# Output product with its engines in a written order, and one load moved a product earlier

## The chip, the cores and the metric

The kernel runs on one core of a Trainium2 chip. The metric is device time in microseconds of one execution of the whole program. Before the change the median of three runs is 2396.21 us, the lowest 2393.97 and the highest 2399.01. Everything is computed in 32-bit floats; matrix products are made of several passes of a faster 32-bit format, as told below.

## The reference

One input `x` of 2048 rows and 1024 columns goes through two branches that a gate per row mixes:

```
g = sigmoid((x * gate_w).sum(-1))
q, k, v = x @ wqkv, 32 heads of 32
phi(t) = [softmax(t @ w_phi), softmax(-(t @ w_phi))]          per head
kv = phi(k)^T v ;  z = sum over rows of phi(k)
o  = phi(q) kv / (phi(q) . z + 1e-6)
a  = o @ wo                                     1024 x 1024
b  = (gelu(x @ w_gate) * (x @ w_up)) @ w_down   1024 -> 3584 -> 1024
out = g * a + (1 - g) * b
```

The last products, `o @ wo` and `h @ w_down`, are summed straight into one output of 2048 x 1024. The kernel scales the attention's rows by `g` before its product, so that product is added with a plain sign, while the MLP's results are scaled by `1 - g` (`g_b`, and `g_n` with the sign turned) in the add.

## The kernel before

A product of two 32-bit matrices is made of three matmuls. Each operand is split into a *high* part (ScalarE copies it into the matmul's format; helper `high`, or the first line of `split`) and a *low* part (VectorE subtracts the high part from the original; `low`, or the second line of `split`); the passes are high x high, high x low and low x high (`PASSES`). So before an operand of 128 x 1024 can be used it needs one load by SyncE's DMA queue (SP), one ScalarE instruction and one VectorE instruction.

The kernel has three stages. The first projects keys and values and accumulates `kv` and `z`. The second, the **unit stage**, makes the queries, gates and ups. The third, the **output product**, multiplies with `wo` and `w_down`.

*Unit stage* (lines 438 to 949). Rows are taken in two halves of 1024. A unit is two 128-column blocks of one weight matrix (kind g, u or q) against one half. It is done as seven products of 12 matmuls (as in Strassen's scheme) with operands that are sums of blocks; they are called x, y, z and v on the weight side. `unit` emits one product per slot, and after each product `run_slot(t)` lets generators emit other engines' work. A generator yields (earliest slot, deadline, VectorE cost, ScalarE cost); among those that may go, the one with the earliest deadline goes first, and without a passed deadline it goes only while the slot's budget of 2.65 us lasts. All of TensorE, VectorE, ScalarE and SP stand in this written order. Staging buffers are taken in a rotation of four by `hold`, and `room(n)` says whether the next n are free.

`weights` is the generator for one unit's weight operands. Sums of weight blocks ("T sums") are made in the first half, stored by `right_sums` in memory, and read back in the second half: the first of them with the unit's first loads, the second (line 597, tile names tq, tg and tu) with a yield of its own on line 594. `second_half` replaces the x operands while the halves change; its loads (line 521) have four staging buffers and are read back from `xs` or from the input. `first_rights` prepares the first two right operands of the output product in the last unit.

*Output product* (lines 952 to 1037). For each of seven products `i` (in the order `ORDER`), first the attention part (2 steps of the contraction per half of the rows), then the MLP part (7 steps per half). A *turn* is one product for one half and one part: four accumulation banks, filled over 2 or 7 steps. A *step* is 24 matmuls: a left operand of 128 x 1024 (high and low) against a right operand of 128 x 1024 (high and low), in four row blocks. There are 28 turns and 126 steps. The order of the two halves alternates, so that a right operand is used in two turns.

- `left` (line 985) loads one block or two into `stage` and `sl`, adds or subtracts them on VectorE (line 992), and splits the result into one of three slots: two named wgu and one named wl.
- `right` (line 957) does the same with rows of `wo` or `w_down`, staged in three buffers named sr, into one of ten slots (three named tyz, seven named tw). `make_right` makes at most one per step, in the MLP part at every other step.
- `add_into` (line 1000) empties the banks of a finished turn: with ScalarE copies the first time a block of the output is reached (line 1007), else with VectorE adds (lines 1010 and 1012), all of them marked urgent. Where a block is finished, it is stored (line 1014).

In this stage only TensorE's order is written (`manual_schedule(engines={PE})`). The order on VectorE, ScalarE and SP is chosen by the framework's planner, which may also move work ahead into the end of the unit stage, and which puts urgent instructions first. Banks alternate between two sets of four: a turn needs the banks of the turn two before it to be empty.

Of the kernel before, what the change touches and what calls it, by code (L numbers as in the profile page):

```python
# [8 lines left out]
F32 = mybir.dt.float32  # L9
F32R = mybir.dt.float32r  # L10
# [6 lines left out]
P = 128  # L17
# [14 lines left out]
def tile_gated_mix(ctx: ExitStack, tc: tile.TileContext, x, xT, wkT, wqT, wv, w_phi, wo,  # L32
# [9 lines left out]
    def split(dst_h, dst_l, src):  # L42
        nc.scalar.activation(dst_h, src, AF.Copy)  # L43
        nc.vector.tensor_tensor(dst_l, src, dst_h.bitcast(F32), OP.subtract)  # L44

    def stage(*parts, pool=None, into=None):
        t = into
        if t is None:
            t = (pool or ring).tile([P, 1024], F32, tag="stage", name="stage", bufs=1 if pool else 3)
        for o, n, src in parts:  # L50
            nc.sync.dma_start(t[:, o:o + n] if len(src.shape) == 2 else
                              t[:, o:o + n].rearrange("p (a b) -> p a b", a=src.shape[1]), src)
        return t
# [7 lines left out]
    def urgent():  # L61
        return tc.high_priority(offset=URGENT)
# [370 lines left out]
    def right_block(src, at, d):  # L433

        r, c = at
        return src[4 * d * P:4 * (d + 1) * P, c * BLK:(c + 1) * BLK].rearrange("(m r p) n -> r p m n", r=2, p=P)[r]

    with tc.tile_pool(name="xa", bufs=1) as xa, tc.tile_pool(name="fp", bufs=1) as fp, \
# [8 lines left out]
        def start(gen):  # L447
            streams.append([next(gen), len(streams), gen])
# [98 lines left out]
        def weights(n, half, kind, m):  # L547
# [369 lines left out]
        def first_rights(t):  # L917

            for d in range(N_ATT):
                yield t + 1 + 3 * d, t + 1 + 3 * d, 0.0  # L920
                while not room(2):
                    yield now[0] + 1, now[0] + 1, 0.0
                a, *b = RIGHT[ORDER[0]]
                k1, s1 = hold((0, 1024, right_block(wo, a, d)))
                k2, s2 = hold((0, 1024, right_block(wo, b[0], d)))
                yield max(now[0] + 2, t + 3 + 4 * d), t + 7, 1.25, 1.05
                w = slot().rearrange("p a b c -> p a (b c)")
                nc.vector.tensor_tensor(s1, s1, s2, OP.add if b[1] == 1 else OP.subtract)
# [4 lines left out]
                made.append(w.rearrange("p a (m n) -> p a m n", m=2))  # L933

        jobs = []
        for n, (half, kind, m) in enumerate(units):
            if n:
# [2 lines left out]
                jobs += [(7 * (n + 1) + 3, half, 2 * m + i // 2, i % 2) for i in range(4)]  # L940
        start(background(jobs, 7 * next(n for n, u in enumerate(units) if u[0])))
        start(first_rights(7 * len(units) - 7))
        start(late_lows())
        for n, u in enumerate(units):
            unit(n, *u, units[n - 1] if n else None)
# [4 lines left out]


    fours = [ctx.enter_context(tc.tile_pool(name=f"po{n}", bufs=4, space=PSUM)) for n in range(2)]
    with tc.tile_pool(name="op", bufs=1) as op, tc.manual_schedule(engines={PE}):
        acc = [ring.tile([P, 4, D], F32, name=f"x{n // 2}{n % 2}", bufs=1) for n in range(4)]
        SLOTS, MID = N_MLP, 3

        def right(src, i, d, pool, tag, bufs):

            w = pool.tile([P, 2, 2, BLK], F32R, tag=tag, name=tag, bufs=bufs)
            a, *b = RIGHT[i]  # L960
            s = stage_right((0, 1024, right_block(src, a, d)))
            if b:
                t = stage_right((0, 1024, right_block(src, b[0], d)))
                nc.vector.tensor_tensor(s, s, t, OP.add if b[1] == 1 else OP.subtract)  # L964
            split(w[:, 0].rearrange("p a b -> p (a b)"), w[:, 1].rearrange("p a b -> p (a b)"), s)
            return w

        def stage_right(*parts):
            t = op.tile([P, 1024], F32, tag="sr", name="sr", bufs=3)
            for o, n, src in parts:  # L970
                nc.sync.dma_start(t[:, o:o + n].rearrange("p (a b) -> p a b", a=src.shape[1]), src)
            return t

        def make_right():

            k = len(made)
            if k < len(rights) and k < used + MID + SLOTS:
                mlp, i, d = rights[k]
                pool, tag, bufs = (mid, "tyz", MID) if k % (MID + SLOTS) < MID else (op, "tw", SLOTS)
                made.append(right(w_down if mlp else wo, i, d, pool, tag, bufs))  # L980

        slots = itertools.cycle((new_weight, new_weight,
                                 lambda: op.tile([P, 2, KC, P], F32R, tag="wl", name="wl", bufs=1)))

        def left(src, i):

            a, *b = LEFT[i]
            s = stage((0, 1024, src[a]))
            if b:
                t = op.tile([P, 1024], F32, tag="sl", name="sl", bufs=2)  # L990
                nc.sync.dma_start(t.rearrange("p (a b) -> p a b", a=2), src[b[0]])
                nc.vector.tensor_tensor(s, s, t, OP.add if b[1] == 1 else OP.subtract)  # L992
            w = next(slots)().rearrange("p a b c -> p a (b c)")
            split(w[:, 0], w[:, 1], s)
            return w.rearrange("p a (m n) -> p a m n", m=2)

        def banks(n):
            return [fours[1 - n % 2].tile([P, BLK], F32, tag="po", name="po") for _ in range(4)]

        def add_into(i, half, ps, mlp, done, last):  # L1000
            for r, col, sign in INTO[i]:
                for c in range(4):
                    row = half * 8 + r * 4 + c
                    part = acc[row // 4][:, row % 4, col * BLK:(col + 1) * BLK]
                    with urgent():
                        if (half, r, col) not in done:
                            nc.scalar.activation(part, ps[c], AF.Copy, scale=float(sign))
                        elif mlp:
                            gate_c = (g_b if sign == 1 else g_n)[:, row:row + 1]
                            nc.vector.scalar_tensor_tensor(part, ps[c], gate_c, part, op0=OP.mult, op1=OP.add)  # L1010
                        else:
                            nc.vector.tensor_tensor(part, part, ps[c], OP.add if sign == 1 else OP.subtract)
                    if (r, col) in last:
                        nc.sync.dma_start(out[row * P:(row + 1) * P, col * BLK:(col + 1) * BLK], part)
                done.add((half, r, col))

        done = set()
        turn = used = 0
        for n, i in enumerate(ORDER):
            for mlp, lefts, n_duo in ((0, left_att, N_ATT), (1, left_mlp, N_MLP)):  # L1020
                last = {t[:2] for t in INTO[i]} - {t[:2] for j in ORDER[n + 1:] for t in INTO[j]} if mlp else set()
                first = used
                for second, half in enumerate((0, 1) if turn % 4 == 0 else (1, 0)):
                    ps = banks(turn)
                    turn += 1
                    for d in range(n_duo):
                        ls = left(lefts[half][d], i)
                        if not mlp or (second * n_duo + d) % 2 == 0:
                            make_right()
                        for m in range(2):  # L1030
                            for c in range(4):
                                for k, (a, e) in enumerate(PASSES):
                                    nc.tensor.matmul(ps[c], ls[:, a, m, c * P:(c + 1) * P], made[first + d][:, e, m],  # L1033
                                                     start=d == 0 and m == 0 and k == 0,
                                                     stop=d == n_duo - 1 and m == 1 and k == 2)
                        used += second
                    add_into(i, half, ps, mlp, done, last)


# [33 lines left out]
```

## Time and profile before

| what | value |
|---|---|
| median of three runs | 2396.21 us |
| the profiled execution's own time | 2396.52 us |
| its span, first to last instruction | 2394.7 us |
| TensorE busy | 2378.0 us, 99% |
| VectorE busy | 1746.9 us, 73% |
| ScalarE busy | 991.4 us, 41% |
| GpSimd busy | 141.6 us, 6% |
| output product, first to last matmul start | 1697.08 to 2390 us |

Times in rows are microseconds from the span's start. A row of the timeline has the start, the time taken, the engine (SPq and POOLq are queues that issue transfers), the line of the kernel, the operation, written tile <- read tiles, shapes, and the count of merged instructions; in brackets, how long the engine was idle before it and what ended that. Matmuls are pipelined: each record lasts about 389 ns, and the next begins before it ends.

### The profile page before, as it was taken

Reading aid. Unit: us, or ns where it says so; the run is one execution under the profiler, and the core shown is the slowest. Engines: PE = TensorE matmul, PEld = TensorE weight load, DVE = VectorE, ACT = ScalarE, POOL = GpSimd, SP = SyncE. Lnnn points to the kernel's source line nnn. Section 1 sums busy time; section 2 is a strip of 40 time slices with the busy share of each in tenths; the row PEclk is TensorE's granted clock in tenths of the full one; section 3 lists DMA queues with packets and bytes.
Section 4 is the critical chain, followed back from the end, with each engine's and each line's share of the span. In section 5 each row is a group of like instructions: output and inputs, shape, how many; then the busy total and the mean of one; then the engine's idle time right before and its main releaser. Section 6 shows DMA issues by size and latency. Waiting matters only on the chain.

```text
span 2394.7 us, 28170 instructions
## 1 busy us (share of the span) xinstructions
PE 2378.0 (99%) x10689; PEld 1973.8 (82%) x10689; DVE 1746.9 (73%) x2183; ACT 991.4 (41%) x1286; POOL 141.6 (6%) x266
## 2 busy tenths in 40 slices
PE   9999999999999999999999999999999999999999
PEld 8888888788888888878888888888887888888887
DVE  7877868857777777877767676777565778677773
ACT  4323332435445444555555555555433323223221
POOL 0000000011111112100000000000000000000000
PEclk9999999999999999999999999999999999999999
DMA  5112333544544566474444444434686667878873
GB/s 178 45 47 86 97 115 100 183 171 144 184 171 142 189 217 225 155 255 138 137 138 156 142 133 139 150 133 141 236 278 205 234 229 271 297 277 290 282 261 131
DMA packets 154360, 425.10 MB, mean 178 GB/s; under 512 B 21360, under 2 KB 21360, under 8 KB 154224
## 3 DMA queue, kind: packets, MB, share of 16 engines
q1 hardware_dynamic: 127872, 336.64, 42.4%
q0 software_dynamic: 25312, 86.52, 9.4%
q8 instruction: 84, 1.38, 0.2%
q14 instruction: 52, 0.43, 0.1%
q10 hardware_dynamic: 1040, 0.13, 0.0%
HBM read 328.34 MB, written 94.90 MB: 177 GB/s over the span
## 4 chain that ended last, share of the span: by engine, by line
PE 71%; DMA 4%; issue 3%; DVE 2%; ACT 0%; POOL 0%; SPq 0%; DVEq 0%; POOLq 0%; ACTq 0%
PE po L1033 24%; PE a L744 19%; PE c L744 13%; PE p L744 6%; PE b L744 6%; DMA sr<-in_w_down 2%; PE misc L906 2%; DVE sr L964 1%; DMA sr<-in_wo 1%; DVE x L1010 1%; DMA stage<-tq 0%; DMA raw<-xs 0%; POOL lm L135 0%; DVE tyz L424 0%; DMA lm<-h 0%
## 5 line engine op out<-in xcount | busy, mean ns | idle before, releaser
L200 PE MATMUL pd<-wkv,x 128*128 128x512 f32 x1536 | 362.0, 393 | 0.0
L200 PEld LDWEIGHTS pd<-wkv,x 128*128 128x128 f32 x1536 | 285.4, 188 | 58.2 <-issue 1.0
L1033 PE MATMUL po<-tw,wgu 128*128 128x512 f32 x1344 | 310.1, 389 | 1.0 <-DVE wgu L44 1.0
L1033 PEld LDWEIGHTS po<-tw,wgu 128*128 128x128 f32 x1344 | 252.3, 188 | 53.6 <-DVE wgu L44 1.4
L43 ACT ACTIVATE wgu<-stage 128x1024 fp32r<-128x1024 f32 x87 | 92.1, 1059 | 237.2 <-PE po L1033 180.8
L744 PE MATMUL a<-s,tyz 128*128 128x512 f32 x744 | 181.2, 392 | 3.1 <-DVE tyz L424 1.6
L424 DVE TENSOR_TENSOR tyz<-stage,tyz 128x1024 fp32r<-128x1024 f32 x126 | 153.0, 1214 | 41.5 <-ACT tyz L421 41.5
L421 ACT ACTIVATE tyz<-stage 128x1024 fp32r<-128x1024 f32 x126 | 132.6, 1052 | 120.3 <-DVE stage L569 65.3
L744 PE MATMUL p<-s,tyz 128*128 128x512 f32 x744 | 178.7, 389 | 0.0
L744 PE MATMUL b<-s,tyz 128*128 128x512 f32 x744 | 178.7, 389 | 0.0
L744 PE MATMUL c<-x,tyz 128*128 128x512 f32 x744 | 178.7, 389 | 0.0
L744 PE MATMUL a<-x,wgu 128*128 128x512 f32 x744 | 178.7, 389 | 0.0
L744 PE MATMUL c<-x,wgu 128*128 128x512 f32 x744 | 178.7, 389 | 0.0
L744 PE MATMUL a<-s,v 128*128 128x512 f32 x744 | 178.7, 389 | 0.0
L992 DVE TENSOR_TENSOR stage<-stage,sl 128x1024 f32<-128x1024 f32 x90 | 109.8, 1225 | 86.1 <-DMA stage<-lm 58.9
L744 PEld LDWEIGHTS a<-s,tyz 128*128 128x128 f32 x744 | 140.4, 189 | 34.2 <-DVE tyz L424 2.9
L744 PEld LDWEIGHTS p<-s,tyz 128*128 128x128 f32 x744 | 139.6, 188 | 29.0
L744 PEld LDWEIGHTS a<-s,v 128*128 128x128 f32 x744 | 139.7, 188 | 29.0
L744 PEld LDWEIGHTS c<-x,wgu 128*128 128x128 f32 x744 | 139.7, 188 | 29.0
L744 PEld LDWEIGHTS c<-x,tyz 128*128 128x128 f32 x744 | 139.7, 188 | 29.0
L744 PEld LDWEIGHTS a<-x,wgu 128*128 128x128 f32 x744 | 139.7, 188 | 29.0
L744 PEld LDWEIGHTS b<-s,tyz 128*128 128x128 f32 x744 | 139.7, 188 | 29.0
(176 smaller groups left out, 3556.0 us busy)
## 6 DMA issues: line engine op xcount, KB each, us to landing
stage<-lm SPq DMA_DIRECT2D x98, 512.0 KB, 4.5
sr<-in_w_down SPq DMA_DIRECT2D x84, 512.0 KB, 4.9
sl<-lm SPq DMA_DIRECT2D x70, 512.0 KB, 4.6
lm<-h POOLq DMA_DIRECT2D x112, 256.0 KB, 2.5
stage<-in_w_gate SPq DMA_DIRECT2D x43, 512.0 KB, 4.2
stage<-in_w_up SPq DMA_DIRECT2D x43, 512.0 KB, 4.3
stage<-la SPq DMA_DIRECT2D x28, 512.0 KB, 4.8
tg<-stage POOLq DMA_DIRECT2D x26, 512.0 KB, 3.0
```

Of the source, the lines that this page charges most:

```text
L43: nc.scalar.activation(dst_h, src, AF.Copy)
L200: nc.tensor.matmul(ps[m], xb[b, kc // 4][:, a, kc % 4, t * P:(t + 1) * P], w[:, e, m * 512:(m + 1) * 512], start=kc == 0 and i == 0, stop= ...
L421: nc.scalar.activation(dst, src, AF.Copy)
L424: nc.vector.tensor_tensor(dst, src, dst_h.bitcast(F32), OP.subtract)
L744: nc.tensor.matmul(dst, w[:, h, 4 * part + kc, :], xq[:, e, kc, :], start=first and kc == 0 and i == 0, stop=kc == 3 and i == 2, skip_grou ...
L906: nc.tensor.matmul(po, kbs[:, a, s, :], pts[:, q, s, :], start=s == 0 and i == 0, stop=s == 1 and i == 2)
L964: nc.vector.tensor_tensor(s, s, t, OP.add if b[1] == 1 else OP.subtract)
L992: nc.vector.tensor_tensor(s, s, t, OP.add if b[1] == 1 else OP.subtract)
L1010: nc.vector.scalar_tensor_tensor(part, ps[c], gate_c, part, op0=OP.mult, op1=OP.add)
L1033: nc.tensor.matmul(ps[c], ls[:, a, m, c * P:(c + 1) * P], made[first + d][:, e, m], start=d == 0 and m == 0 and k == 0, stop=d == n_duo - ...
```

## The change

Two things are changed.

In `weights`, the second T sum of a unit that is not fresh may be loaded from three products ahead of its unit, with a deadline two ahead, where it was two and one.

The output product is rewritten so that TensorE, VectorE, ScalarE and SP all stand in a written order, step by step. A new generator `first_lefts` prepares the first two left operands in the last unit of the unit stage, beside `first_rights`. Before the loop, the loads of lefts 2 to 4 and of two rights are issued. Then each step emits its 24 matmuls and after them: the sum and the high part of the left for two steps later, a load of a left's second term for four steps later, the first right's sum and high part, two adds, the left's low part and the load of a left for five steps later, the rights' remaining parts with two adds between them and one right's load each, and the adds that remain. What a step takes on is chosen by a budget of 5.3 us of VectorE time per step (a wide operation counts 1.25, an add 0.75, a ScalarE copy nothing) and by deadlines: a right must be made two steps before its first use, and a finished turn's adds must be out in the last step before its banks return. A right whose load was issued less than two steps ago is left for later unless it is due. The rights' staging has four buffers where it had three; the three slots of lefts start with wl; adds go bank by bank.

```diff
             if not fresh:
-                yield max(now[0], t - 2), t - 1, 0.0
+                yield max(now[0], t - 3), t - 2, 0.0
...
+        def first_lefts(t):
+            for d in range(2):
+                yield t + 2 + 3 * d, t + 3 + 3 * d, 0.0
+                while not room(1):
+                    yield now[0] + 1, now[0] + 1, 0.0
+                k1, s1 = hold((0, 1024, left_att[0][d][LEFT[ORDER[0]][0]]))
+                yield max(now[0] + 2, t + 4 + 5 * d), t + 7 + 3 * d, 0.0, 1.05
+                w = new_weight()
+                high(flat(w)[0], s1)
+                yield now[0] + 1, now[0] + 1, 1.25
+                low(flat(w)[1], s1, flat(w)[0])
+                held[k1] = False
+                ready.append(Ready(w))
...
-    with tc.tile_pool(name="op", bufs=1) as op, tc.manual_schedule(engines={PE}):
+    with tc.tile_pool(name="op", bufs=1) as op, tc.manual_schedule(engines={PE, DVE, ACT, SP}):
...
+            t = op.tile([P, 1024], F32, tag="sr", name="sr", bufs=4)
...
+        for n in range(2, 5):
+            lefts[n].load()
+        for n in range(2, 4):
+            lefts[n].load_other()
+        for r in todo[:2]:
+            r.load(-1)
...
+            owed = min(owed, 0.0) + STEP
+            nxt = lefts[n + AHEAD] if n + AHEAD < len(steps) else None
+            if nxt:
+                owed -= nxt.cost
+            adds, preps = [], []
+            while True:
+                r = todo[len(preps)] if len(preps) < len(todo) else None
+                if r and (made_of(r.k) > n or r.when >= n - 1 and needed[r.k] - 2 > n):
+                    r = None
+                last_r = needed[r.k] - 2 if r else 10 ** 9
+                last_a = waiting[len(adds)][0] if len(adds) < len(waiting) else 10 ** 9
+                if min(last_r, last_a) == 10 ** 9 or (owed <= 0 and min(last_r, last_a) > n):
+                    break
+                if last_a <= last_r:
+                    a = waiting[len(adds)]
+                    owed -= 0.0 if a[1][6] else 0.75
+                    adds.append(a)
+                else:
+                    owed -= r.cost
+                    preps.append(r)
...
+            if nxt:
+                nxt.first()
+                if n + AHEAD + 2 < len(steps):
+                    lefts[n + AHEAD + 2].load_other()
+            for r in preps[:1]:
+                r.first()
+            some(2)
+            if nxt:
+                nxt.second()
+                if n + AHEAD + 3 < len(steps):
+                    lefts[n + AHEAD + 3].load()
+            for q, r in enumerate(preps):
+                if q:
+                    r.first()
+                    some(2)
+                r.second()
+                if unloaded:
+                    unloaded.pop(0).load(n)
+            some(len(adds))
+            if closes:
+                waiting += [(begins[turn + 2] - 1, a, ps[a[4]]) for a in turns[turn]]
```

Here `first` is the sum (if there are two terms) and the high part, `second` the low part, `some(n)` up to n of the step's adds, `STEP` 5.3, `AHEAD` 2, and `made_of(k)` the first step in which a right's slot is free.

More of the change, by code (lines that the diff above doesn't have):

```diff
@@ L933, in first_rights, with __init__ @@
                 made.append(w.rearrange("p a (m n) -> p a m n", m=2))
+        ready = []
+        def first_lefts(t):
[11 more added lines that the diff above has]
+                ready.append(Ready(w))
+        class Ready:
+            def __init__(self, w):
+                self.out = w.rearrange("p a b c -> p a (b c)").rearrange("p a (m n) -> p a m n", m=2)
         jobs = []
@@ L942, in tile_gated_mix @@
         start(first_rights(7 * len(units) - 7))
+        start(first_lefts(7 * len(units) - 7))
         start(late_lows())
@@ L952, in tile_gated_mix @@
     fours = [ctx.enter_context(tc.tile_pool(name=f"po{n}", bufs=4, space=PSUM)) for n in range(2)]
-    with tc.tile_pool(name="op", bufs=1) as op, tc.manual_schedule(engines={PE}):
+    with tc.tile_pool(name="op", bufs=1) as op, tc.manual_schedule(engines={PE, DVE, ACT, SP}):
         acc = [ring.tile([P, 4, D], F32, name=f"x{n // 2}{n % 2}", bufs=1) for n in range(4)]
[L955 to L971, printed above, removed]
-            return t
[L974 to L1001, printed above, removed]
-                for c in range(4):
[L1003 to L1037, printed above, removed]
@@ new lines, in tile_gated_mix @@
+        turns, steps, lefts, freed, needed = [], [], [], {}, {}
+        done = set()
+        for n, i in enumerate(ORDER):
+            for mlp, srcs, n_duo in ((0, left_att, N_ATT), (1, left_mlp, N_MLP)):
+                last = {t[:2] for t in INTO[i]} - {t[:2] for j in ORDER[n + 1:] for t in INTO[j]} if mlp else set()
+                base = rights.index((mlp, i, 0))
+                for second, half in enumerate((0, 1) if len(turns) % 4 == 0 else (1, 0)):
+                    adds = [(half, r, col, sign, c, mlp, (half, r, col) not in done, (r, col) in last)
+                            for c in range(4) for r, col, sign in INTO[i]]
+                    done |= {(half, r, col) for r, col, _ in INTO[i]}
+                    for d in range(n_duo):
+                        (freed if second else needed)[base + d] = len(steps)
+                        steps.append((len(turns), d, base + d, d == 0, d == n_duo - 1))
+                        lefts.append(ready[len(lefts)] if len(lefts) < len(ready) else Left(srcs[half][d], i))
+                    turns.append(adds)
@@ new lines, in tile_gated_mix @@
+        begins = [next(n for n, s in enumerate(steps) if s[0] == t) for t in range(len(turns))] + [len(steps)] * 2
+        made_of = lambda k: (-1 if k < MID + SLOTS else freed[k - MID - SLOTS]) + 1
+        todo = [Right(k) for k in range(len(made), len(rights))]
+        waiting, banks_of, owed = [], {}, 0.0
+        AHEAD = 2
+        for n in range(2, 5):
[4 more added lines that the diff above has]
+            r.load(-1)
@@ new lines, in tile_gated_mix, with some @@
+        unloaded = todo[2:]
+        for n, (turn, d, k, opens, closes) in enumerate(steps):
+            if opens:
+                banks_of[turn] = [fours[1 - turn % 2].tile([P, BLK], F32, tag="po", name="po") for _ in range(4)]
+            ps, ls, rs = banks_of[turn], lefts[n].out, made[k]
+            for m in range(2):
+                for c in range(4):
+                    for j, (a, e) in enumerate(PASSES):
+                        nc.tensor.matmul(ps[c], ls[:, a, m, c * P:(c + 1) * P], rs[:, e, m],
+                                         start=opens and m == 0 and j == 0, stop=closes and m == 1 and j == 2)
+            owed = min(owed, 0.0) + STEP
[15 more added lines that the diff above has]
+                    adds.append(a)
+                else:
+                    owed -= r.cost
+                    preps.append(r)
+            del waiting[:len(adds)], todo[:len(preps)]
+            def some(count):
+                for _, a, bank in [adds.pop(0) for _ in range(min(count, len(adds)))]:
+                    add_into(*a[:5], bank, *a[5:])
+            if nxt:
[19 more added lines that the diff above has]
+                waiting += [(begins[turn + 2] - 1, a, ps[a[4]]) for a in turns[turn]]
@@ L1041 @@
+        for _, a, bank in waiting:
+            add_into(*a[:5], bank, *a[5:])
 def kernel(A_x, A_wqkv, A_w_phi, A_wo, B_x, B_w_gate, B_w_up, B_w_down, gate_w):
```

57 lines of the change are left out of this document (added).

## The prediction

> **What bounds the kernel now.** I read the page's busy shares first, then TensorE's waits over the whole span.
>
> ```profile
> span 2394.7 us, 28170 instructions
> PE 2378.0 (99%) x10689; PEld 1973.8 (82%) x10689; DVE 1746.9 (73%) x2183; ACT 991.4 (41%) x1286; POOL 141.6 (6%) x266
> PE po L1033 <- DVE wl L44: 3.6, 1, 3.6
> ```
>
> TensorE is the bound, and the change removes no matmul; the longest of its waits, 3.6 us, lies at line 1033, the output product. So a gain can only be time in which TensorE waits or runs slowly. The next view is TensorE's timeline in the output product.
>
> ```profile
> 1697.08 11.04 PE L1033 MATMUL po<-tyz,wgu 128*128 128x512 f32 x48
> ...
> 1762.36 6.05 PE L1033 MATMUL po<-tw,wgu 128*128 128x512 f32 x26
> 1769.38 5.29 PE L1033 MATMUL po<-tw,wgu 128*128 128x512 f32 x22 [0.96 <-DVE wgu L44]
> ...
> 1779.94 11.04 PE L1033 MATMUL po<-tw,wgu 128*128 128x512 f32 x48
> ...
> 1801.70 5.60 PE L1033 MATMUL po<-tyz,wgu 128*128 128x512 f32 x24
> 1808.02 0.70 PE L1033 MATMUL po<-tw,wl 128*128 128x512 f32 x2 [0.71 <-ACT wgu L43]
> 1812.35 6.86 PE L1033 MATMUL po<-tw,wl 128*128 128x512 f32 x22 [3.64 <-DVE wl L44]
> 1819.05 11.04 PE L1033 MATMUL po<-tyz,wgu 128*128 128x512 f32 x48
> ...
> 2384.81 5.60 PE L1033 MATMUL po<-tyz,wl 128*128 128x512 f32 x24
> ```
>
> The undisturbed pace is the difference of two rows: 48 matmuls at 1779.94 take 11.04 us, 24 at 1801.70 take 5.60, so 24 more cost 5.44 us, 0.2267 each; 24 are a step. The output product runs from 1697.08 to 2384.81 + 5.60 = 2390.41, 693.33 us. Its loops make 7 x 18 steps of 24, 3024 matmuls, 685.44 us at that pace, plus 0.16 us by which the last record outlasts its pace. **7.73 us are lost.** Two places hold all of it: 1762.36 to 1779.94 is 17.58 us for 72 matmuls worth 16.32 (1.26 lost), and 1801.70 to 1819.05 is 17.35 us for 48 worth 10.88 (6.47 lost).
>
> The same reading at the start of the unit stage's second half:
>
> ```profile
> 1056.39 2.88 PE L744 MATMUL c<-x,tyz 128*128 128x512 f32 x12
> 1060.30 0.73 PE L744 MATMUL a<-s,tyz 128*128 128x512 f32 x2 [1.03 <-ACT c L777]
> 1062.21 3.99 PE L744 MATMUL a<-s,tyz 128*128 128x512 f32 x10 [1.18 <-DVE tyz L424]
> ...
> 1066.04 2.88 PE L744 MATMUL a<-s,v 128*128 128x512 f32 x12
> ```
>
> 1056.39 to 1066.04 is 9.65 us for two products of 12, worth 5.44: **4.21 us lost.** Not all of it is waiting: the ten matmuls at 1062.21 take 3.99 us where their pace gives 2.43, 1.56 us more. The windows view of TensorE says why (columns after the window: its length, PE busy, granted clock, DMA share, GB/s):
>
> ```profile
> 1062.00:1065.50 3.50, 3.29 (x8) 0.52 0.76 256
> 1812.40:1815.80 3.40, 3.40 (x9) 0.57 0.67 196
> ```
>
> After the waits the granted clock falls to 0.52, and to 0.57 after the one at 1812. A wait of 1 us alone (1769.38) was not followed by such a spell.
>
> The Trainium skill, "TensorE: Matmul & The Clock Gate", part 1, has the clock fall to half "after ≥1 idle window (~3.4µs)" of a free-running window. Here 2.21 us of gaps inside 3.4 us were enough, so the measurement decides: by that rule a new wait of 2 us would cost 2 us, by these rows up to 3.56.
>
> **The change, part by part.**
>
> *(a) Adds spread over steps.* What makes the long stall is visible on VectorE and ScalarE:
>
> ```profile
> 1805.81 1.41 DVE L1010 SCALAR_TENSOR_TENSOR x<-po,g_b,x 128x512 f32<-128x512 f32 x2
> ...
> 1811.08 1.22 DVE L44 TENSOR_TENSOR wl<-stage,wl 128x1024 fp32r<-128x1024 f32 x1
> 1807.84 3.99 ACT L1007 ACTIVATE x<-po 128x512 f32<-128x512 f32 x8
> ```
>
> Eight urgent adds (5.27 us, 0.66 each) stand ahead of the low half of the left operand that the current step needs; the wait at 1769.38 has the same make-up. In the new program a left's low half stands behind at most two adds (1.32 us), it is for two steps later (the three slots free one at the beginning of each step), and the adds have until their banks return. Counting VectorE work per step, with 1.22 us for a wide operation:
>
> ```profile
> L992 DVE TENSOR_TENSOR stage<-stage,sl 128x1024 f32<-128x1024 f32 x90 | 109.8, 1225 | 86.1 <-DMA stage<-lm 58.9 <-DMA stage<-la 14.3 <-DMA sl<-lm 6.2
> ```
>
> a left with two terms costs 2.45, a right with two terms 2.45, four adds 2.64: the heaviest steady steps come to 5.1 to 5.5 us of the 5.44, followed by lighter ones; the early steps 1, 3, 5, 7 and 9 hold a one-term left and two rights, 6.1 us, each followed by 1.2. Nothing accumulates beyond one step, and a left has one step (5.44) in hand. I take both stalls as gone: -7.73. Bounds: -7.73 and, if one stall of the long kind stays, -1.26.
>
> *(b) The order at the beginning* is where I see a price. Queues are now in written order and the output pool still opens only when the last spill has been read:
>
> ```profile
> 1697.89 1.22 DVE L424 TENSOR_TENSOR tyz<-stage,tyz 128x1024 fp32r<-128x1024 f32 x1
> 1699.02 0.68 DVE L719 TENSOR_TENSOR h<-a,x 128x512 f32<-128x512 f32 x1
> 1700.73 0.54 POOL L135 DMA_DIRECT2D lm<-h  x1 [1.92 <-DVE h L721]
> 1703.99 1.41 SPq L971 DMA_DIRECT2D sr<-in_w_down  x3
> 1704.05 1.06 ACT L43 ACTIVATE wl<-stage 128x1024 fp32r<-128x1024 f32 x1 [0.22 <-ACT wgu L43]
> 1705.14 1.22 DVE L44 TENSOR_TENSOR wl<-stage,wl 128x1024 fp32r<-128x1024 f32 x1
> 1709.49 1.23 DVE L964 TENSOR_TENSOR sr<-sr 128x1024 f32<-128x1024 f32 x1 [3.12 <-DMA sr<-in_w_down]
> ```
>
> The second early left's low half falls between the right's low (1697.89) and the unit's last subtraction (1699.02), by the deadlines in the code. Wide operations follow each other by 1.13 us there, so the spill goes at 1701.86, the loads of the rights at 1705.12 and step 2's left is complete at 1707.5; TensorE wants it at 1707.96. The first right's sum comes 5.5 us after its load, 1710.6; behind it, in order, the left of step 3 (done 1713.0, wanted 1713.40), the two rights' remaining halves, the left of step 4 (1718.7, wanted 1718.84), and on ScalarE the eight copies of turn 0 from 1717.3, 0.50 each, to 1721.3. Turn 2 wants their banks at 1718.84, 1719.52, 1720.20 and 1720.88: the last comes 0.4 late. I take **+0.5**. Bounds: 0 (the low half falls behind the subtraction), and +2.8, if the first loads take 7.8 us, as the load in the next fence does, in place of 5.5.
>
> *(c) The second T sums.*
>
> ```profile
> 1045.49 0.46 SPq L51 DMA_DIRECT2D stage<-in_w_up  x1
> 1046.08 1.22 DVE L424 TENSOR_TENSOR tyz<-stage,tyz 128x1024 fp32r<-128x1024 f32 x1
> 1048.46 1.46 SPq L521 DMA_DIRECT2D x<-xs  x2
> 1049.97 0.42 SPq L51 DMA_DIRECT2D stage<-tq  x1
> 1057.76 1.06 ACT L421 ACTIVATE tyz<-stage 128x1024 fp32r<-128x1024 f32 x1 [3.89 <-DMA stage<-tq]
> 1060.94 1.22 DVE L424 TENSOR_TENSOR tyz<-stage,tyz 128x1024 fp32r<-128x1024 f32 x1
> ```
>
> The load at 1049.97 takes 7.8 us; ScalarE stands in it for 3.89 us, and behind that instruction are the copy L777 and the half that VectorE finishes, the two releasers of the stall. One slot earlier, the load's deadline is ahead of those of the two x<-xs loads, so on SP it passes them and goes right behind the one at 1045.49, about 4 us earlier; its buffer is that of four holds back, long free. The passed loads move by one issue, 0.4 us; their highs come after 1060. The stall needs 2 us to vanish: -4.21. In the other units no wait is seen on these loads; the cover is the product by which they already come early. Bounds: -4.21 and 0.
>
> *(d) Loads of rights* gather: in the longest bursts a step fetches a two-term left and a two-term right, four transfers of 0.524 MB, 2.10 MB in 5.44 us or 385 GB/s.
>
> ```profile
> 2100.00:2133.00 33.00, 33.00 (x148) 27.32 (x147) 27.95 (x32) 8.27 (x8) 0.00 (x0) 1.00 0.91 324
> 2200.00:2250.00 50.00, 50.00 (x223) 41.40 (x222) 38.78 (x41) 12.62 (x12) 0.00 (x0) 1.00 0.83 285
> sr<-in_w_down SPq DMA_DIRECT2D x84, 512.0 KB, 4.9
> ```
>
> 324 GB/s at a share of 0.91 is 356 at full share; 2.10 MB then takes 5.89 us, 0.45 over, 1.8 us after a run of four. A right's load has two steps less some 3.5 us, 7.4, against the median 4.9: 2.5 us in hand. So 0; the other bound is the slow rival below.
>
> *(e) The end.*
>
> ```profile
> 2388.41 2.79 DVE L1010 SCALAR_TENSOR_TENSOR x<-po,g_b,x 128x512 f32<-128x512 f32 x4 [11.91 <-PE po L1033]
> ```
>
> The last four adds and stores stay as they are: 0.
>
> **Sum**: 2394.74 - 7.73 - 4.21 + 0.5 = 2383.3 us of span. The profiled execution took 2396.52, 1.8 more than its span, and lies 0.31 above the median 2396.21: 2385.1, so **2384.8 for the median**.
>
> **The rivals.**
> 1. *The early load gains nothing* (it is written behind the second operand's low half and may still come out behind the x<-xs loads): 2384.8 + 4.21 = 2389.0. For it: one generator emits them in sequence. Against: that low half (VectorE, 1046.08) precedes the x<-xs loads.
> 2. *A new stall in the output product*: the start's margins of 0.1 to 0.5 us fail, or a bank's adds come late: 2.3 us (2387.1) up to one stall like that at 1808 (6.47, 2391.3). For it: a right's sum that waits for its transfer now blocks adds and lefts behind it. Against: a step in hand everywhere but at the start.
> 3. *Slower: the bursts become bound by transfers.* At 285 GB/s, 2.10 MB takes 7.37 us, 1.93 over a step. Three runs of three or four such steps, 11 in all, lose 21.2 us less 2.5 in hand for each, 13.7; with a slow spell (1.56) each, 18.4: 2403.2. It is slower than before once the rate in the bursts falls under some 312 GB/s (1.29 over, 11 x 1.29 - 7.5 + 4.7 = 11.4). For it: the 285 above. Against: 324 sustained for 33 us below full share.
>
> **How the numbers follow.** Forecast (all stalls gone, 0 to 2.3 new at the start) 0.62; rival 1 0.12; rival 2 0.17; rival 3 0.06; anything else 0.03. 0.2% is 4.8 us, what a measurement here can tell: faster is below 2391.4. That is the forecast, rival 1 and a third to a half of rival 2, 0.80; the rest of rival 2 with some of "anything else", 0.13, is the same; rival 3 and the remainder, 0.07, slower. Low end: floor 2384.3 (no new loss) less most of what the runs before spread below their median (2.2), 2382.5. High end: rival 2's top with most of that spread, 2393. The likeliest alone: 2383.5 to 2387.5.
>
> **What would show it.** (a) No TensorE gap over 0.3 us after step 12 of the output product, adds in pairs between lefts. (b) The sr loads about 1 us later than 1703.99 relative to the stage's begin, step 2 and 3 barely served, a gap under 1 us at turn 2. (c) stage<-tq ahead of the x<-xs loads, ScalarE without the 3.89 us, granted clock 1.00 there. (d) DMA slices near 350 GB/s without TensorE waits. Wrong is the forecast if waits on sr transfers reach TensorE in the bursts, or if the output product takes more than 688 us from its first matmul to its last.

## The result and the profile after

The changed kernel takes 2384.03 us (median of five runs, 2383.34 to 2384.63) against 2396.21 (five, 2393.06 to 2399.01): a ratio of 0.995, 95% interval 0.9935 to 0.9965, 12.2 us faster. The forecast was 2384.8. The profiled execution took 2383.34 us. The page and TensorE's waits:

```profile
span 2381.5 us, 28170 instructions
PE 2372.2 (100%) x10689; PEld 1969.3 (83%) x10689; DVE 1746.3 (73%) x2183; ACT 991.6 (42%) x1286; POOL 142.2 (6%) x266
...
PE c L703 <- DVE h L651: 1.6, 1, 1.6
...
PE a L744 <- DVE tyz L424: 0.4, 1, 0.4
PE a L744 <- ACT c L777: 0.4, 1, 0.4
```

No wait at the output product stands in this view any more; the rows that remain lie in the first 665 us, which the change does not touch. TensorE's timeline in the output product (line 1088 is what line 1033 was):

```profile
1691.01 11.04 PE L1088 MATMUL po<-tyz,wgu 128*128 128x512 f32 x48
1701.89 5.60 PE L1088 MATMUL po<-tyz,wl 128*128 128x512 f32 x24
1707.33 11.57 PE L1088 MATMUL po<-tyz,wgu 128*128 128x512 f32 x48
1718.74 5.60 PE L1088 MATMUL po<-tw,wl 128*128 128x512 f32 x24
...
2371.54 5.60 PE L1088 MATMUL po<-tyz,wl 128*128 128x512 f32 x24
```

From 1691.01 to 2371.54 + 5.60 it takes 686.13 us where it took 693.33. The one loss is at 1707.33: 11.41 us to the next row for 48 matmuls worth 10.88, **0.53 us**. The start of the second half:

```profile
1043.98 0.46 SPq L51 DMA_DIRECT2D stage<-in_w_up  x1
1044.49 0.42 SPq L51 DMA_DIRECT2D stage<-tq  x1
1046.96 1.46 SPq L521 DMA_DIRECT2D x<-xs  x2
1052.62 1.05 ACT L421 ACTIVATE tyz<-stage 128x1024 fp32r<-128x1024 f32 x1
1054.51 2.88 PE L744 MATMUL c<-x,tyz 128*128 128x512 f32 x12
1057.23 2.88 PE L744 MATMUL a<-s,tyz 128*128 128x512 f32 x12
```

The load of tq passes the two x<-xs loads, ScalarE no longer stands in it, and the products follow at their pace of 2.72 us. Between the same marks of the two timelines:

| stretch | before | after | difference |
|---|---|---|---|
| to the first unit product | 464.20 | 462.69 | -1.51 |
| on to the product c at the second half's start | 592.19 | 591.82 | -0.37 |
| on to the first output matmul | 640.69 | 636.50 | -4.19 |
| output product | 693.33 | 686.13 | -7.20 |
| last matmul to the end | 4.33 | 4.33 | 0 |

The first two rows are not the change. The first comes from the first 20 us, where one execution runs a few more matmuls slowly than another:

```profile
9.17 2.31 PE L200 MATMUL pd<-wkv,x 128*128 128x512 f32 x6
```
```profile
8.19 1.64 PE L200 MATMUL pd<-wkv,x 128*128 128x512 f32 x6
```

The first fence is before, the second after. In another profile of the changed kernel, after_again below, the first unit product begins at 464.23, as before.

### The profile page after: what moved, and what is told of

Read it like the earlier page. It is cut to its first block, busy times and chain, and to the rows that moved or that the text cites. A ratio compares the mean times of both kernels' runs of the same rounds, so it can differ in the third digit from the quotient of the medians.

```text
span 2381.5 us, 28170 instructions
## 1 busy us (share of the span) xinstructions
PE 2372.2 (100%) x10689; PEld 1969.3 (83%) x10689; DVE 1746.3 (73%) x2183; ACT 991.6 (42%) x1286; POOL 142.2 (6%) x266
## 4 chain that ended last, share of the span: by engine, by line
PE 79%; DVE 0%; ACT 0%; issue 0%; ACTq 0%; DVEq 0%
PE po L1088 29%; PE a L744 21%; PE c L744 14%; PE b L744 7%; PE p L744 7%; PE misc L906 2%; DVE x L1048 0%; ACT L872 0%; DVE x L888 0%; DVE tyz L424 0%; ACT x L872 0%; DVE st L876 0%; DVE x L879 0%; ACT tyz L421 0%; DVE v L424 0%
## 5 line engine op out<-in xcount | busy, mean ns | idle before, releaser
L421 ACT ACTIVATE wgu<-stage 128x1024 fp32r<-128x1024 f32 x147 | 155.2, 1057 | 291.0 <-PE po L1088 225.1
L424 DVE TENSOR_TENSOR wgu<-stage,wgu 128x1024 fp32r<-128x1024 f32 x147 | 179.6, 1222 | 123.7 <-ACT wgu L421 123.5
```

The source lines that it names most:

```text
L421: nc.scalar.activation(dst, src, AF.Copy)
L424: nc.vector.tensor_tensor(dst, src, dst_h.bitcast(F32), OP.subtract)
```

## The experiments

Each kernel is timed beside runs of the kernel before on the same chip; "before" is their median there. Gains in the text are differences of these medians; in brackets behind some of them stands what the interval of the ratio makes of it in us.

| kernel | median, us (lowest to highest) | before | ratio, 95% |
|---|---|---|---|
| z_alone | 2392.58 (2391.04 to 2395.16) | 2396.20 | 0.9978 to 0.9996 |
| out_alone | 2387.12 (2386.12 to 2389.87) | 2396.20 | 0.9953 to 0.9978 |
| after_again | 2383.72 (2383.32 to 2385.27) | 2396.20 | 0.9939 to 0.9964 |
| one_right | 2383.11 (2382.72 to 2384.58) | 2396.20 | 0.9936 to 0.9961 |
| sr4_only | 2390.57 (2387.08 to 2396.19) | 2397.56 | 0.9963 to 0.9982 |
| no_urgent | 2396.14 (2394.47 to 2398.82) | 2397.56 | 0.9986 to 1.0005 |
| bunch | 2383.70 (2383.46 to 2385.15) | 2397.56 | 0.9931 to 0.9961 |
| bunch_lead1 | 2390.05 (2389.58 to 2392.55) | 2397.56 | 0.9963 to 0.9982 |
| lead1 | 2389.97 (2388.41 to 2391.56) | 2396.08 | 0.9965 to 0.9984 |
| no_early_lefts | 2383.43 (2383.26 to 2383.57) | 2396.08 | 0.9931 to 0.9961 |
| extra_loads | 2383.61 (2383.25 to 2383.95) | 2396.08 | 0.9931 to 0.9964 |
| two_small | 2387.17 (2384.26 to 2390.25) | 2398.07 | 0.9943 to 0.9967 |

### The two parts alone

z_alone is the kernel before with

```diff
-                yield max(now[0], t - 2), t - 1, 0.0
+                yield max(now[0], t - 3), t - 2, 0.0
```

> The kernel before with only the earlier load of the second T sums. My theory: the stall at the start of the second half (4.2 us by the timeline) goes, nothing else changes: about 2392.0 against 2396.2, the output product keeps its 7.7 us. Rival: that stall is an accident of the one profiled execution, and the median moves by less than 1 us; or the gain is given back in the units that follow, whose loads are moved too.

out_alone is the changed kernel with that line as before.

> The changed kernel with the second T sums loaded as before. My theory: the output product from its first to its last matmul takes some 686 us in place of 693.3, the stall at the start of the second half stays: about 2389 against 2396.2, 7.2 us faster. Rival: the two parts are not independent, and this one alone gives under 5 or over 10 us.

after_again is the changed kernel unaltered.

> The changed kernel, beside its two parts on the same chip. My theory: its gain is the sum of the two parts' gains within 1 us, 11.4 us and up to 12.2. Rival: the parts overlap, and the sum is more than 2 us off.

The early load alone gives 3.6 us (1.0 to 5.3), the output product alone 9.1 (5.3 to 11.3), both 12.5, and the sum of the parts is 12.7: they add up. The 9.1 are more than the 7.73 that before's profile has to give there, but the interval holds both. TensorE's waits in z_alone and in out_alone, one fence each:

```profile
PE po L1033 <- DVE wl L44: 4.5, 2, 3.6
```
```profile
PE a L744 <- ACT c L777: 2.3, 2, 1.9
PE a L744 <- DVE tyz L424: 1.5, 2, 1.0
```

Each keeps the other's stall. The stall at the second half's start is not of one size: out_alone's longest wait for L777 is 1.9 us, where before had 1.0, and with the slow matmuls behind it its profile loses 6.2 us there (14.32 us for 36 matmuls worth 8.16), where before lost 4.21. After_again's output product takes 685.60 us, with nothing lost, not even the 0.53.

### What made the long stall: the burst or the transfers

In the kernel before, VectorE's row just ahead of the burst of adds is a right's sum that waited for its transfer:

```profile
1801.07 1.23 DVE L44 TENSOR_TENSOR tw<-sr,tw 128x1024 fp32r<-128x1024 f32 x1
1804.67 1.23 DVE L964 TENSOR_TENSOR sr<-sr 128x1024 f32<-128x1024 f32 x1 [2.37 <-DMA sr<-in_wo]
```

The adds behind it belong to a turn that ended 9.5 us earlier: the step that TensorE begins at 1801.70 is the second after that turn, which puts the turn's end about 1796.3. They were ready; they stood behind the sum. The load that the sum waited for went out just as the sum before it ended, at 1799.94, which frees one of the three buffers:

```profile
1798.71 1.23 DVE L964 TENSOR_TENSOR sr<-sr 128x1024 f32<-128x1024 f32 x1 [2.08 <-DMA sr<-in_w_down]
1799.96 0.37 SPq L971 DMA_DIRECT2D sr<-in_wo  x1
```

Two edits of the kernel before were to tell the two causes apart. sr4_only:

```diff
-            t = op.tile([P, 1024], F32, tag="sr", name="sr", bufs=3)
+            t = op.tile([P, 1024], F32, tag="sr", name="sr", bufs=4)
```

> The kernel before, its planner's order kept, with four staging buffers for rights where it has three. Theory P: the stalls of the output product come from rights whose transfers are issued late for want of a buffer; VectorE stands in their sums, in front of the adds and of the left's low half. With four the stalls shrink: 5 to 7 us faster than before (2389 to 2391). Theory U: the burst of eight urgent adds alone makes them; then nothing changes (2396) and the long wait at the seventh of the early turns stays near 6.5 us.

no_urgent:

```diff
-                    with urgent():
-                        if (half, r, col) not in done:
+                    if (half, r, col) not in done:
```

> The kernel before without the mark of urgency on the adds and copies that empty the banks. Theory U: the planner no longer puts eight adds ahead of the left's low half, both stalls shrink, 4 to 7 us faster. Theory P: the order changes but VectorE still stands in the rights' sums; as long or longer, since banks now come free later: 2396 to 2402.

**With the fourth buffer the stalls are gone from the profile, and the burst alone does not make them.** sr4_only's only edit is the buffer; it gives 7.0 us (4.3 to 8.9), and its profiled execution spends 685.60 us in the output product, with nothing lost. no_urgent can't be told from before, but it does not test theory U as it was meant to: without the mark, the planner still puts the eight adds between the sum and the low half.

```profile
1804.38 1.23 DVE L964 TENSOR_TENSOR sr<-sr 128x1024 f32<-128x1024 f32 x1 [1.92 <-DMA sr<-in_wo]
1805.53 2.72 DVE L1009 SCALAR_TENSOR_TENSOR x<-po,g_b,x 128x512 f32<-128x512 f32 x4
1808.16 2.72 DVE L1009 SCALAR_TENSOR_TENSOR x<-po,g_n,x 128x512 f32<-128x512 f32 x4
1810.80 1.22 DVE L44 TENSOR_TENSOR wl<-stage,wl 128x1024 fp32r<-128x1024 f32 x1
```

In its profile TensorE still waits for that low half, and for an add besides:

```profile
PE po L1032 <- DVE wl L44: 3.2, 2, 1.9
PE po L1032 <- DVE x L1009: 2.5, 1, 2.5
```

What speaks against the burst alone is sr4_only. There the burst of eight adds is still in its place ahead of the low half, but everything stands earlier:

```profile
1797.40 1.23 DVE L964 TENSOR_TENSOR sr<-sr 128x1024 f32<-128x1024 f32 x1 [1.53 <-DMA sr<-in_wo]
1798.55 1.41 DVE L1010 SCALAR_TENSOR_TENSOR x<-po,g_b,x 128x512 f32<-128x512 f32 x2
...
1803.82 1.22 DVE L44 TENSOR_TENSOR wl<-stage,wl 128x1024 fp32r<-128x1024 f32 x1
...
1805.04 5.60 PE L1033 MATMUL po<-tw,wl 128*128 128x512 f32 x24
```

The low half ends at 1805.04, the moment at which the step begins; its first use is the step's third matmul, 0.45 us later. So this execution had no stall, with 0.45 us in hand.

From the start of the sum to the end of the low half 7.6 us pass in both kernels, 5.27 of them in the burst. The low half is wanted 5.89 us after the step ahead of its own begins (5.44 and the 0.45). So the sum must begin at least 1.7 us before that step ahead does. In sr4_only it begins 2.20 us before it (the step begins at 1799.60), in before 2.97 us after it (1801.70), and in z_alone, with three buffers and the same stall, 2.92 us after it, though VectorE waits there only 1.44 us ahead of the sum, less than sr4_only's 1.53. So the length of that one wait tells nothing; the time at which the sum begins does. The sum's load went out 5.97 us ahead of the step in sr4_only (1793.63), and 1.74 us ahead of it in before.

The burst has its part all the same. Without its 5.27 us before's low half would have been done at about 1807.0, ahead of the 1807.6 at which it was wanted; that is an estimate from these rows, and no run tests it. And the planner answered the fourth buffer with another order in places: around the long stall VectorE's order is the same as before's, while at the first one the sum that stood just ahead of the burst (1761.69) no longer stands there. What the buffer gives with the order held fixed was not run.

### Spread adds, and the lead of a left

bunch is the changed kernel with all adds of a finished turn at once, ahead of the next left's low half:

```diff
-            adds, preps = [], []
+            adds, preps = waiting[:], []
+            owed -= sum(0.0 if a[1][6] else 0.75 for a in adds)
...
-            some(2)
+            some(len(adds))
             if nxt:
                 nxt.second()
```

> The changed kernel, but all adds of a finished turn go in one burst in the step after it, ahead of the low half of the left for two steps later. If it is the two steps of lead that removed the stalls, nothing happens: the burst of 5.3 us and the low half of 1.2 end 6.5 us into the step, and the left is wanted after 10.9: within 1 us of the changed kernel. If it is the spreading of the adds, the stalls come back: at each turn with eight VectorE adds some 1 us or more, 8 us or more in all.

Nothing happens: 2383.70. With four buffers and two steps of lead, the stalls stay away without the spreading. bunch_lead1 and lead1 prepare a left one step ahead, with bursts and without:

```diff
-        AHEAD = 2
+        AHEAD = 1
...
-            nxt = lefts[n + AHEAD] if n + AHEAD < len(steps) else None
+            nxt = lefts[n + AHEAD] if 2 <= n + AHEAD < len(steps) else None
```

> The same bursts, and a left is prepared one step ahead of its use, not two. The burst and the low half then end 6.5 us into a step of 5.44: by the theory of the lead TensorE waits 0.6 to 1.1 us at each of some 16 turns with eight VectorE adds, 10 to 18 us slower than the changed kernel. If neither lead nor spreading matters, no change.

> The changed kernel with lefts prepared one step ahead and the adds spread as they are. At most two adds (1.3 us) stand ahead of a low half (1.2), 2.5 us of a step of 5.44: by my count no new stall, within 1 us of the changed kernel. If the lead alone removed the stalls, several us slower.

Both miss: lead1 was to cost nothing and costs 6.3 us more than after_again, bunch_lead1 was to cost 10 to 18 and takes as long as lead1. In both, nearly the whole difference is one stall in the third step. lead1's rows on VectorE, then TensorE:

```profile
1705.34 1.23 DVE L1005 TENSOR_TENSOR sr<-sr 128x1024 f32<-128x1024 f32 x1 [8.44 <-DMA sr<-in_w_down]
1706.48 1.22 DVE L424 TENSOR_TENSOR wl<-stage,wl 128x1024 fp32r<-128x1024 f32 x1
...
1703.30 0.61 PE L1088 MATMUL po<-tyz,wl 128*128 128x512 f32 x2
1707.76 8.04 PE L1088 MATMUL po<-tyz,wl 128*128 128x512 f32 x22 [3.84 <-DVE wl L424]
```

The left of step 2 is now written behind the first right's sum, and VectorE stands 8.44 us in that sum's transfer. Everywhere else in these two profiles one step is enough, even with the bursts. My count of 6.5 us had the burst begin when the turn ends. bunch_lead1's rows, VectorE then TensorE, show where it begins:

```profile
1758.98 0.75 DVE L1048 SCALAR_TENSOR_TENSOR x<-po,g_b,x 128x512 f32<-128x512 f32 x1 [3.36 <-PE po L1088]
...
1764.26 1.22 DVE L424 TENSOR_TENSOR wgu<-stage,wgu 128x1024 fp32r<-128x1024 f32 x1
...
1760.82 5.60 PE L1088 MATMUL po<-tyz,wl 128*128 128x512 f32 x24
1766.26 9.00 PE L1088 MATMUL po<-tw,wgu 128*128 128x512 f32 x39
```

The four banks finish one after the other, so the first add begins 1.84 us before the next turn's first matmul, and the low half is done at 1765.5, 0.8 us before its step begins.

### The beginning

no_early_lefts takes the generator for the first two lefts away and writes their preparation at the head of the output product (the three slots of lefts then start with the two named wgu):

```diff
-        start(first_lefts(7 * len(units) - 7))
...
-        for n in range(2, 5):
-            lefts[n].load()
+        for n in range(3):
+            lefts[n].load()
+        for n in range(2):
+            lefts[n].first()
+            lefts[n].second()
+            lefts[n + 3].load()
```

> The changed kernel without the generator that prepares the first two lefts in the last unit; they are prepared at the head of the output product's written order instead, which the planner no longer moves ahead. TensorE should wait at the first output matmul: VectorE's last subtraction of the unit stage begins some 2.7 us after that matmul's time, the low half follows it, about 3.5 to 5 us in all, and more where the second left and the rights shift behind: 4 to 7 us slower than the changed kernel. Rival: the planner's moving ahead did not matter, since the matmuls with the high part can go first: under 1 us.

The loss of 4 to 7 us did not come: 2383.43. ScalarE's timeline shows why; the two high parts still go into the last unit, between instructions that are written before them:

```profile
1677.06 1.06 ACT L421 ACTIVATE wgu<-stage 128x1024 fp32r<-128x1024 f32 x1 [1.25 <-DMA stage<-la]
1678.03 0.58 ACT L779 ACTIVATE b<-a 128x512 f32<-128x512 f32 x1
...
1683.79 1.06 ACT L421 ACTIVATE wgu<-stage 128x1024 fp32r<-128x1024 f32 x1 [1.08 <-PE c L744]
```

So work at the head of a stage with a written order is still moved ahead into the stage before, and neither the expectation nor its rival was put to the test.

one_right makes at most one right per step in the first ten steps:

```diff
-                if r and (made_of(r.k) > n or r.when >= n - 1 and needed[r.k] - 2 > n):
+                if r and (n < 10 and preps or made_of(r.k) > n or r.when >= n - 1 and needed[r.k] - 2 > n):
```

> The changed kernel, but with at most one right operand per step in the first ten steps, where it made two in every other. My theory: the 0.5 us that TensorE loses at the third turn comes from the eight ScalarE copies, which stand behind the high part of the second of two rights; with that right a step later they begin about 1 us earlier and the loss goes: 0.5 us faster than the changed kernel, seen in TensorE's timeline rather than in the time. Rival: the copies are held by the first right's transfer, and the loss stays or moves to the lefts of steps 3 to 5.

The copies of turn 0, in after, after_again and one_right, a fence each:

```profile
1711.16 3.99 ACT L1045 ACTIVATE x<-po 128x512 f32<-128x512 f32 x8
```
```profile
1712.70 3.99 ACT L1045 ACTIVATE x<-po 128x512 f32<-128x512 f32 x8
```
```profile
1710.28 4.00 ACT L1045 ACTIVATE x<-po 128x512 f32<-128x512 f32 x8
```

Counted from the first output matmul (1691.01, 1693.45, 1691.41) they end at 24.1, 23.2 and 22.9 us; the last bank is wanted at 23.8. Of the three only the first is late, by 0.3 us, and only that profile loses time there, 0.53 us; in out_alone the copies end at 23.8 and 0.20 is lost. The four fit the copies as the cause, but no run changes the copies alone. Whether they are late differs between executions of one kernel, and one_right's gain on after_again (0.6 us, overlapping ranges) is not shown to come from this: after_again lost nothing there.

### Transfers in the bursts

extra_loads adds a copy of a left's block in memory to the steps in which loads gather:

```diff
+                if 60 <= n < 72 or 96 <= n < 108:
+                    xt = dram.tile([P, 2, BLK], F32, name=f"xt{n}")
+                    nc.sync.dma_start(xt, nxt.src[nxt.at[0]])
```

> The changed kernel with one more transfer of 0.524 MB per step (a block of a left copied in memory, read by nobody) in steps 60 to 71 and 96 to 107, where the rights' loads gather: 2.62 MB in the heaviest steps, 7.4 us of transfer at 356 GB/s, 1.95 us over a step. My theory: four such steps lose 7.8 us, of which 2.5 are in hand in the rights' loads and 5.4 in the lefts: no stall or one under 1 us. Rival, that the bursts have little in hand: 5 us or more in each of the two runs of steps, 10 us slower or more.

No stall at all. The windows view of the first heavy run of steps, in after and then in extra_loads (the last two columns are the DMA share and GB/s):

```profile
2056.00:2078.00 22.00, 22.00 (x98) 18.20 (x97) 18.67 (x17) 8.05 (x8) 0.00 (x0) 1.00 0.96 355
```
```profile
2056.00:2078.00 22.00, 22.00 (x99) 18.22 (x98) 18.17 (x16) 8.20 (x8) 0.00 (x0) 1.00 1.02 398
```

TensorE is busy throughout in both. With the extra copies VectorE waits 8.1 us in all for rights over both runs of steps (none in after), and nothing of it reaches TensorE.

### Both small edits without the written order

two_small is the kernel before with the edits of z_alone and sr4_only.

> The kernel before with two small edits: four staging buffers for rights, and the second T sums loaded a product earlier. The output product's order on VectorE, ScalarE and SP stays with the planner. If the fourth buffer is what removed the output product's stalls, the gains add up: 7.0 from the one and 3.6 from the other, 2385 to 2386, or 2384 as the changed kernel, with no TensorE wait over 0.5 us after the first unit. If the written order does more than that, this one stays 2 us or more behind the changed kernel.

It lies between, at 2387.17, with runs from 2384.26 to 2390.25. The 10.9 us that it gains are about the sum of the two edits' gains, 7.0 and 3.6. Its profiled execution is the slowest of them, and the long stall is back (VectorE, then TensorE):

```profile
1797.18 1.23 DVE L964 TENSOR_TENSOR sr<-sr 128x1024 f32<-128x1024 f32 x1 [3.83 <-DMA sr<-in_wo]
...
1803.60 1.21 DVE L44 TENSOR_TENSOR wl<-stage,wl 128x1024 fp32r<-128x1024 f32 x1
...
1804.86 8.04 PE L1033 MATMUL po<-tw,wl 128*128 128x512 f32 x22 [3.05 <-DVE wl L44]
```

The sum's load, in two_small and then in sr4_only:

```profile
1791.11 0.37 SPq L971 DMA_DIRECT2D sr<-in_wo  x1
```
```profile
1793.63 0.37 SPq L971 DMA_DIRECT2D sr<-in_wo  x1
```

In two_small it goes out 4.64 us ahead of the step that begins at 1795.75, and the sum begins 6.07 us later; in sr4_only it went out 5.97 us ahead and the sum began 3.77 us later. Both differences together, 3.6 us, put the sum 1.43 us behind the step's beginning, and the 0.45 us in hand did not cover that. So the planner's order can reach the changed kernel's time and does not hold it; sr4_only's ten runs likewise reach from 2387.08 to 2396.19, as slow as before. In the medians its 10.9 us stand against 12.5 for after_again; the two intervals overlap, so a difference in time between them is not shown. What is shown is the mechanism, in this one execution, and the spread: 6.0 us over six runs, against 2.0 over five of after_again.

The written order with three buffers was not tried. Whether spread adds and two steps of lead would have removed the stalls without the fourth buffer stays open.

## Why the prediction was right, step by step

**(a) The output product, -7.73: the size right, the cause half right, and so in part by luck.** 7.20 went in the profile and all 7.73 in after_again. The step said that eight urgent adds ahead of the low half make the stall, and that spreading them and two steps of lead remove it. The burst is 5.27 of the 7.6 us that had to fit, but sr4_only keeps it and loses nothing. What was late was the sum ahead of the burst, whose load had gone out late for want of a buffer. bunch and lead1 show that, once there are four buffers, the spreading is not needed and the lead in the third step alone. The fourth buffer is part of the change, so the size came out; the prediction gives it no place in this step, and sr4_only gets 7.0 us by it. The row was there to be read: a right's sum that waits for its transfer, just ahead of the burst, and begins 2.97 us after the step that it had to be ahead of.

**(b) The beginning, +0.5: right in this execution, by two errors.** The second early left's low half did not go ahead of the unit's last subtraction but behind it, so the pool opened when it used to, and the first loads of rights went 6.53 us after the first output matmul, where it had been 6.91 and about 1 us more was forecast; the first right's sum, taken there as 5.5 us, came 6.95 us after its load, which is one of four now (1697.54 to 1704.49). What the step said of the copies and the last bank fits what happened. As a fixed cost it is wrong: 0.53, then 0 in after_again.

**(c) The T sums, -4.21: right.** The load went right behind the one before it, 5.5 us earlier in the execution (1044.49 against 1049.97, of which some 2 belong to this execution's earlier start), and 4.19 went. In medians it is 3.6 (1.0 to 5.3); the stall differs between executions, as out_alone's 6.2 us shows.

**(d) Gathering loads, 0: right**, and with more in hand than I gave it: 355 GB/s in the heaviest steps without a wait for a right, and 398 in extra_loads, whose copies within memory count in it, above the 356 that I had taken for full share. **(e) The end: right**, 4.33 us in both.

**The rivals.** The first fell with (c), the third with extra_loads. The second did not happen in this kernel; it is what lead1 shows when a left is written behind the first right's sum.

The remaining 1.9 us of the profile's 13.3 lie ahead of the second half and are a matter of the execution, not of the change. Why before spreads over 6 us and the changed kernel over 1.3 is explained in part: its two stalls hang on transfers, and they vary (out_alone, two_small). How much each adds to the spread stays open.

## What to carry to other kernels

When an engine in written or planned order is late, go back along its rows from the late work and ask when each row began and what let it begin; the releaser that a wait names is only the last link. Here the burst took most of the time, and the sum ahead of it had begun too late. Try the buffer before the order: here one more staging buffer gave 7.0 us, and with the written order besides the times spread less from one execution to the next (2.0 us in after_again, 9.1 in sr4_only). A bank's results can be drained while the turn's other banks still fill, so a burst of drains can begin earlier than the turn's end, 1.84 us earlier in bunch_lead1.

## What the runs showed of the hardware that was not expected

Slow spells after waits do not follow the length of one wait alone. The Trainium skill, "TensorE: Matmul & The Clock Gate", part 1, asks for an idle window of some 3.4 us. The runs show less to be enough, and not always, so the measurement decides. Before's two waits of 1.03 and 1.18 us, 0.7 us apart, were followed by a granted clock of 0.52. The wait of 1.6 us at line 703 in after was not: the windows view (its length, PE busy, granted clock, DMA share, GB/s) for the 4 us behind it shows

```profile
467.00:471.00 4.00, 3.70 (x15) 1.00 0.48 172
```

And the spell can cost nearly as much as the wait: after two_small's 3.05 us, TensorE ran at a clock of 0.58 for 7 us, 22 matmuls in 8.04 us whose pace gives 5.15.

```profile
1804.80:1812.00 7.20, 7.14 (x19) 0.58 0.77 252
```
